# Planned attention, Fourier mixing and MLP on one core: the second batch's Y in other PSUM banks, fold scalings and some evacuations on ScalarE, tabled landing times for the loads

## The chip, the cores and the metric

The kernel runs on one core of a Trainium2 chip. The core has five engines with a queue each: TensorE (PE, matmuls, with its weight loads shown apart as PEld), VectorE (DVE), ScalarE (ACT), GpSimd (POOL) and SyncE (SP), which here only issues DMAs. An engine works through its queue in order; engines wait for each other through semaphores. TensorE writes to PSUM, which holds eight banks of 128 partitions x 512 fp32; DVE and ACT read the results out ("evacuate" them).

The metric is the device time in microseconds (us) of the whole kernel, the median over several runs. Seven runs of the kernel before gave 284.14 us as the median, from 281.46 to 285.59. One execution was profiled; it took 282.36 us, of which 280.6 us lie between its first and its last instruction (the span).

## The reference, cut to what matters

Four batches of 768 positions, 8 heads of 64. Attention keeps the first 8 keys and a band of 96; its output `x` is mixed by a two-dimensional Fourier transform of which only the real part is kept, normalised, and sent through a two-layer network:

```
scores = q @ k.T / 8 - slope[h] * dist        # kept: key < 8, or 0 <= i - j < 96
a      = softmax(scores)
x      = (a @ v), heads side by side            # 768 x 512 per batch
mixed  = real(fft(fft(x, axis=seq), axis=model))
u      = x + mixed
un     = (u - mean(u)) / sqrt(var(u) + 1e-6)
out    = u + relu(un @ w_ch1) @ w_ch2           # 512 -> 2048 -> 512
```

## The kernel before, in words

**Stages of a batch.** Eight heads are taken as four pairs `hp`; `n = 4*b + hp` counts pairs over all batches b = 0 to 3. For each pair q and k are loaded (`qs`), cast to fp16 (`qk`, line 398 on ACT, 402 on POOL), transposed on TensorE (`pt`, L487) and evacuated (`qkT`, L493, on DVE). Three score tiles follow (`sc_0` to `sc_2`, L529), each with an exponential on ACT (`er`, L552) and a product with the bias table on DVE (`ex`, L567). v is loaded by two DMAs a pair (`vs`, L360) and cast on POOL (L458). Six products with v (`pav`, L658) are normalised on DVE (L677 and L678) into `x`.

The Fourier transform over the sequence folds x first, on DVE: `f1` (L725, L726) forms sums and differences of the halves, `f2` (L731, L732) a second level, `f3` (L736 to L739) four of six results, the last two of them scalings by a constant, `f4` (L743, L744) the other two. `fold_d` folds over the model dimension: `g1` (L794 to L797) and `g2` (L811 to L822). The second batch's fold is cut into two halves of 256 columns, those of the third and fourth are whole (512). The folded tiles meet DFT matrices in `y_unit`: four groups of products (`py`, L855 to L862), each group in a PSUM tile of two banks, evacuated to `zy` (L875 on ACT, L877 on DVE). `mirror` makes reversed copies (`rev` on POOL, `ww` at L908 on ACT or L910 on POOL). `u_unit` makes three products (`pu`, L942) of pairs of row classes; DVE adds x (L963) and the row sums follow; `un` is the normalised row (L983 ACT, L985 DVE). `nt_unit` transposes it (`ptu`, L1014) and evacuates it (`unT`, L1024 ACT, L1026 DVE).

**The network.** Each batch gives three chunks `c` of 256 rows. A chunk has eight first products (`ph`, L1045, one bank each, evacuated with Relu into `hT` at L1051 on ACT or L1052 on DVE) and two second products (`pg`, L1068, four parts of four matmuls each), which end in `ob` (L1079, DVE) and a store (L1084, issued on ACT or SP).

**PSUM.** After the first batch's attention there are three rings: `xx` with two slots of two banks, for scores, transposes, pav, py, pu and ptu; `ph` with two single banks; `pg` with two single banks.

**What sets the order.** The program is written out by a planner (`Plan`) while it is built. It keeps a clock for each engine and a completion time for each token, in its own estimates (`act(n)`, `dve(n)`, `lat` for the landing of a load), and emits next what can start first, among `MIX`, `ATT`, `PH` and `PG` for TensorE and, for the other engines, among the operations that are ready. An operation with several "ways" goes to the engine that ends it earliest. The result is a fixed order on each queue. A wait that comes out longer on the chip than in the estimates holds everything behind it on that queue. An estimate that is changed moves instructions on all engines, though no operation is touched.

**Loads.** Loads of q and k rotate through three `qs` buffers, those of v through two. Until now a load's token was set to the planner's DMA clock plus a constant per batch: 4.5, 7.0 and 5.0 us for batches 1, 2 and 3.

Of the kernel before, what the change touches and what calls it, by code (L numbers as in the profile page):

```python
# [14 lines left out]
P = 128  # L15
# [160 lines left out]
def kernel(  # L176
# [48 lines left out]
    t0 = []  # L225
# [113 lines left out]
    qk16 = {}  # L339
    TT = {}  # L340

    def load(b, hp, which):
        n = HP * b + hp
        h0 = 2 * hp
        vtag, vi = ("u", hp) if b == 0 else ("vs", n - HP)
        stage[("vs", n)] = (vtag, vi)
        gate = [("hold", b)] if b == 2 else [("xri", 0)] if b == 1 else []
        if which == "v" and b == 0:
            def run():
                t = buf(vtag, vi, [P, 2 * NS, Dh], FP32, 1)  # L350
                stage[("v", n)] = t
                qk_dma(t.rearrange("p (j t) d -> p j (t d)", t=2), v, b, h0)
            pl.later([("SP", 0.45, run)], free(vtag, vi), 0.0, [("ld", "v", n)], dma=1.34)
        elif which == "v":
            def run():
                t = buf(vtag, vi, [P, 2 * NS, Dh], FP32, 1)
                stage[("v", n)] = t
                src = v[b, h0:h0 + 2].rearrange("h s d -> (h s) d").rearrange("(n m t) d -> t m n d", m=64, t=2)
                for t2 in range(2):
                    nc.sync.dma_start(t[64 * t2:64 * t2 + 64], src[t2])  # L360
            pl.later([("SP", 0.9, run)], free(vtag, vi) + gate, 0.0, [("ld", "v", n)], lat=(0.0, 4.5, 7.0, 5.0)[b], dma=2.45)
        elif b == 0 and hp < 3:
            cell = {}

            def run(cell=cell):
                cell[0] = buf("hT", hp, [P, 2, NS, 2 * Dh], FP32, 2)
                for w, src in enumerate((q, k)):
                    qk_dma(cell[0][:, w], src, b, h0)
            pl.later([("SP", 0.9, run)], free("hT", hp), 0.0, [("ld", "qk", n, w) for w in range(2)], dma=2.68,
                     then=lambda t: pl.tok.__setitem__(("ld", "qk", n, 0), t - 1.34))  # L370
            for w in range(2):
                cast_qk(b, hp, w, lambda w=w, cell=cell: cell[0][:, w], ("hT", hp))
        else:
            for w, src in enumerate((q, k)):
                cell = {}
                i = 2 * (n - 3) + w

                def run(cell=cell, src=src, i=i):
                    cell[0] = buf("qs", i, [P, NS, 2 * Dh], FP32, 1)
                    qk_dma(cell[0], src, b, h0)  # L380
                pl.later([("SP", 0.45, run)], free("qs", i) + gate, 0.0, [("ld", "qk", n, w)],
                         lat=(0.0, 4.5, 7.0, 5.0)[b], dma=1.34)
                cast_qk(b, hp, w, lambda cell=cell: cell[0], ("qs", i))

    def qk_dma(t, src, b, h0):
# [92 lines left out]
    def trans(b, hp):  # L478
        n = HP * b + hp

        def run(start, ring):
            pt = bank("xx", f"pt_{n}", FP16)
            src = qk16.pop(n)
            for w in range(2):
                for j in range(NS):
                    o = pt[:, w, (j // 2) * 256:(j // 2) * 256 + 256].rearrange("p (a t m) -> p t a m", a=2, t=2)
                    nc.tensor.transpose(o[:, j % 2], src[:, w, j].rearrange("p h d -> p (h d)"), idn)  # L487
            e = pl.pe(mm_us(P, 2 * NS), start)
            pl.used(("free", "qk", n), e)

            def evac():
                TT[n] = buf("qkT", n, [P, 2, S], FP16, 6)
                V.tensor_copy(TT[n], pt[:, :, 0:S])  # L493
            pl.later([("DVE", dve2(2 * S), evac)], free("qkT", n), e, [("qkT", n)], ring=ring, rank=RA(b))
            for s in range(2):
                def cp(s=s):
                    c0 = 16 * (hp % 2) + 8 * s
                    nc.gpsimd.tensor_copy(  # L498
                        kG[b % 2][64 * s:64 * s + 64, hp, c0:c0 + NG].rearrange("p (j m) -> p j m", j=2),
                        TT[n][64 * s:64 * s + 64, 1, 0:P].rearrange("p (j m) -> p j m", j=2)[:, :, 0:NG // 2])  # L500
                pl.later([("POOL", 0.2, cp)], [("qkT", n)] + ([("gldone", b - 2, hp // 2)] if b > 1 else []), 0.0,
                         [("kG", n, s)], [("free", "qkT", n)], rank=RA(b))
        ATT.append(([("qk", n, 0), ("qk", n, 1)], ("xx",), run))
# [205 lines left out]
    def fold_s(b):  # L709
# [5 lines left out]
        for n, (c0, cw) in enumerate(parts):  # L715
# [10 lines left out]
                VT(ab[:, 1], lo, hi, op=ALU.subtract)  # L726

            def f2(c0=c0, cw=cw, n=n, cell=cell):
                pm = cell["pm"] = buf("ww", IW(b, n), [P, 2, 2, cw], FP16, 1)
                ab = cell["ab"]  # L730
                VT(pm[:, 0], ab[:, :, 1], ab[:, :, 2], op=ALU.add)  # L731
                VT(pm[:, 1], ab[:, :, 1], ab[:, :, 2], op=ALU.subtract)  # L732

            def f3(c0=c0, cw=cw, cell=cell):
                ab, pm, zc = cell["ab"], cell["pm"], T[("z", b)][:, :, c0:c0 + cw]
                VT(zc[:, 0], ab[:, 0, 0], pm[:, 0, 0], op=ALU.add)  # L736
                VT(zc[:, 1], ab[:, 1, 0], pm[:, 1, 1], op=ALU.subtract)
                V.tensor_scalar_mul(zc[:, 4], pm[:, 1, 0], c)
                V.tensor_scalar_mul(zc[:, 5], pm[:, 0, 1], c)  # L739

            def f4(c0=c0, cw=cw, cell=cell):
                ab, pm, zc = cell["ab"], cell["pm"], T[("z", b)][:, :, c0:c0 + cw]
# [5 lines left out]
                     + (free("zy", 2 * b) if n == 0 else []), 0.0,  # L748
                     [("f1", b, n)], [("free", "x", b)] * (2 // len(parts)))
            pl.later([("DVE", 2 * dve2(2 * cw), f2)], [("f1", b, n)] + free("ww", IW(b, n)), 0.0, [("f2", b, n)])  # L750
            pl.later([("DVE", 4 * dve2(cw), f3)], [("f2", b, n)], 0.0, [("f3", b, n)])
            pl.later([("DVE", 2 * dve(cw), f4)], [("f3", b, n)], 0.0, [("z", b, n)],
                     [("free", "eA", IA(b, n)), ("free", "ww", IW(b, n))])
        return [("z", b, n) for n in range(len(parts))]

    def fold_s0():

# [85 lines left out]
    def y_unit(b, g, ts=None):  # L843
        def run(start, ring):
            py = bank(ring, f"py_{b}_{g}" + (f"_{ts[0]}" if ts else ""))
            cnt = 0
            ys = YG[g]
            for a, (rs, rd) in enumerate(ys):
                if ts and a // 2 not in ts:
                    continue  # L850
                o = py[:, a // 2, (a % 2) * 256:(a % 2) * 256 + 256]
                if b == 0:
                    ops = W[(0, rs, rd)]
                    for i, (l, r) in enumerate(ops):
                        nc.tensor.matmul(o, l, r, start=(i == 0), stop=(i == len(ops) - 1))  # L855
                    cnt += len(ops)
                    continue
                wr, wi = W[(b, rs, rd)]
                nc.tensor.matmul(o, wr, t1_sb[:, rs, 128:384], start=True, stop=(wi is None))  # L859
                cnt += 1  # L860
                if wi is not None:
                    nc.tensor.matmul(o, wi, t1_sb[:, rs, 0:256], start=False, stop=True)  # L862
                    cnt += 1
# [6 lines left out]
            def cp(on, lo, hi):  # L870
                if ("y", b) not in T:
                    T[("y", b)] = buf("zy", 2 * b + 1, [P, 8, 2, 2, P], FP16, 7)
                dst = T[("y", b)][:, 2 * g + lo:2 * g + hi].rearrange("p t a c m -> p t (a c m)")
                if on == "ACT":
                    A(dst, py[:, lo:hi, :], AF.Copy)  # L875
                else:
                    V.tensor_copy(dst, py[:, lo:hi, :])  # L877
                for t in range(lo, hi):
                    for a in range(2):
                        Y[(b,) + ys[2 * t + a]] = T[("y", b)][:, 2 * g + t, a]  # L880
            cuts = [(0, nb)] if ts is None else [(t, t + 1) for t in ts]
            for x, (lo, hi) in enumerate(cuts):
# [2 lines left out]
                          ("DVE", dve(w), lambda lo=lo, hi=hi: cp("DVE", lo, hi))],  # L885
                         free("zy", 2 * b + 1), e, [("y", b) + y for y in ys[2 * lo:2 * hi]],
                         CD(b) if x == len(cuts) - 1 else [], ring=ring if x == len(cuts) - 1 else None)
        MIX.append(([("w", b, 0 if g in (0, 3) else 1), ("c", "t1" if b else "t0")], BANKS(b), run))

    def mirror(b):  # L890

# [39 lines left out]
    def u_unit(b, pr):  # L931
# [4 lines left out]
        def run(start, ring):  # L936
# [29 lines left out]
                                           op0=ALU.mult, op1=ALU.add, accum_out=sm[:, a, 0:1])  # L966
                V.tensor_scalar_mul(sm[:, rows[0]:rows[-1] + 1, 1], sm[:, rows[0]:rows[-1] + 1, 0], -SC / Dm)

            cuts = [(0,), (1,)] if c == 0 else [(0, 1)]
            for rows in cuts:  # L970
                last = rows is cuts[-1]
                pl.later([("DVE", len(rows) * dve(512) + 0.15, lambda rows=rows: add(rows))],
# [4 lines left out]
            def un(on, a):  # L977

                if 0 not in cell:
                    cell[0] = T[("un", c)] = buf("un", 1 + c, [P, 2, Dm], FP16, 4 if c == 0 else 3)  # L980
                m = MV[c][:, a, 1:2]
                if on == "ACT":
                    A(cell[0][:, a], UT[c][:, a], AF.Identity, m, SC)  # L983
# [108 lines left out]
    with tc.manual_schedule():  # L1092
# [78 lines left out]
        for b in range(B):  # L1171
# [37 lines left out]
            bounce(b)  # L1209
            fold_d(b, fold_s(b))  # L1210
            for g in (0, 1, 2, 3):
                if b:
                    y_unit(b, g)
                    continue
                for t in range(len(YG[g]) // 2):
                    y_unit(b, g, [t])
                    if (g, t) == (2, 0):
                        u_unit(b, 0)
            mirror(b)
            if b:  # L1220
                u_unit(b, 0)
            u_unit(b, 1)
            for rows in ((0,), (1,)) if b == 0 else ((0, 1),):
                nt_unit(b, 0, rows)
            u_unit(b, 2)
            nt_unit(b, 1)
# [43 lines left out]
```

## Time and profile before

| what | value |
|---|---|
| median of 7 runs | 284.14 us (281.46 to 285.59) |
| profiled execution | 282.36 us, span 280.6 us |
| busy: PE, DVE, ACT, POOL | 265.1, 180.8, 145.7, 58.9 us |
| of it `ph` and `pg` matmuls | 95.1 and 90.7 us |
| chain that ended last | PE 78% of the span |
| granted TensorE clock | mean 0.991; 0.5 from 111.8 to 115.2 us |
| last matmul ends, span ends | 276.5 us, 280.6 us |

Busy PE is not PE at its peak: the ends of matmuls are modelled and overlap. What tells more is the time from one group of matmuls to the next. Undisturbed, eight `ph` matmuls take 0.87 us, four `pg` 0.86, sixteen `pu` 0.89, eight `ptu` 0.45, twelve `pt` 0.67 and four `sc` about 0.42. Where a group takes longer, or the next starts late, TensorE has lost time.

### The profile page before, as it was taken

How to read it: one execution, taken by the hardware profiler on the slowest of the kernel's cores; microseconds unless marked ns; L12 is line 12 of the kernel's file. 1: busy time of each engine (PE TensorE's matmuls, PEld its weight loads, DVE VectorE, ACT ScalarE, POOL GpSimd, SP SyncE). 2: the span in 40 equal slices, each digit the busy share in tenths (PEclk: the TensorE clock that was granted, in tenths of full speed). 3: DMA queues.
4: the chain of work that ended last, by engine and by line, in shares of the span. 5: the costliest groups of instructions: out<-in, count | busy, mean ns of one | idle time of the engine just before them, and what ended most of it. 6: DMA issues, size and time to landing. Idle time of an engine off the chain costs nothing.

```text
span 280.6 us, 6105 instructions
## 1 busy us (share of the span) xinstructions
PE 265.1 (94%) x2505; PEld 179.0 (64%) x2505; DVE 180.8 (64%) x363; ACT 145.7 (52%) x236; POOL 58.9 (21%) x115
## 2 busy tenths in 40 slices
PE   7788899899999996999999999999999899999994
PEld 3445587688675454776795576775866677767441
DVE  4675938677599978777899687575995672111121
ACT  2877347886741258668534267686142556434000
POOL 1572625154023323340111011111000120100000
PEclk9999999999999999799999999999999999999998
DMA  7999789999999999634047102000352010000111
GB/s 219 292 278 288 176 254 200 217 232 206 248 195 278 295 269 229 135 106 114 1 103 219 72 2 78 0 2 2 98 158 83 2 71 8 37 37 20 58 75 75
DMA packets 63101, 38.10 MB, mean 136 GB/s; under 512 B 20450, under 2 KB 58594, under 8 KB 62946
## 3 DMA queue, kind: packets, MB, share of 16 engines
q1 hardware_dynamic: 51458, 25.66, 38.4%
q10 hardware_dynamic: 7392, 7.87, 9.1%
q0 software_dynamic: 4224, 4.19, 9.1%
q8 instruction: 19, 0.31, 0.5%
q14 instruction: 8, 0.07, 0.1%
HBM read 32.47 MB, written 9.44 MB: 149 GB/s over the span
## 4 chain that ended last, share of the span: by engine, by line
PE 78%; SPq 7%; DMA 7%; DVE 4%; ACT 1%; issue 1%; ACTq 0%
PE ph L1045 31%; PE pg L1068 29%; SPq L387 5%; PE sc L529 4%; DMA qs<-in_q_dram 3%; PE pav L658 3%; PE pt L487 3%; DMA gb<-gbm 2%; PE pu L942 2%; PE ptu L1014 2%; DVE x L678 2%; PE py L859 2%; DVE u L963 1%; SPq L360 1%; PE py L862 1%; DMA xd<-x 1%
## 5 line engine op out<-in xcount | busy, mean ns | idle before, releaser
L1045 PE MATMUL ph<-unT,w 128*128 128x256 f16 x768 | 95.1, 274 | 1.1 <-ACT hT L1051 1.1
L1068 PE MATMUL pg<-w,hT 128*128 128x512 f16 x384 | 90.7, 379 | 0.0
L1045 PEld LDWEIGHTS <-w 128*128 128x128 f16 x768 | 71.9, 98 | 18.0 <-issue 6.9
L1068 PEld LDWEIGHTS <-hT 128*128 128x128 f16 x384 | 36.5, 98 | 35.7 <-issue 1.0
L1051 ACT ACTIVATE hT<-ph 128x512 f16<-128x512 f32 x60 | 35.7, 596 | 44.6 <-PE ph L1045 40.2
L552 ACT ACTIVATE er<-sc 128x992 f16<-128x992 f32 (+2 forms) x42 | 38.1, 924 | 14.2 <-PE sc L529 12.4
L1079 DVE SCALAR_TENSOR_TENSOR ob<-pg,sm,u 128x512 f32<-128x512 f32 x24 | 18.0, 750 | 37.7 <-PE pg L1068 34.5
L1052 DVE TENSOR_SCALAR hT<-ph 128x512 f16<-128x512 f32 x36 | 24.7, 689 | 19.4 <-PE ph L1045 19.4
L567 DVE TENSOR_TENSOR ex<-er,mk 128x992 f16<-128x992 f16 (+2 forms) x42 | 26.7, 652 | 2.3 <-ACT er L552 2.3
L398 ACT ACTIVATE qk<-qs 128x768 f16<-128x768 f32 x20 | 16.6, 838 | 17.7 <-DVE ob L1079 5.6
L963 DVE SCALAR_TENSOR_TENSOR u<-pu,xr 128x512 f32<-128x512 f32 x24 | 15.7, 687 | 8.7 <-PE pu L942 8.6
L493 DVE COPY qkT<-pt 128x1536 f16<-128x1536 f16 x16 | 15.3, 954 | 3.9 <-PE pt L487 3.7
L875 ACT ACTIVATE zy<-py 128x1024 f16<-128x1024 f32 (+1 forms) x11 | 9.1, 826 | 16.6 <-DVE eA L811 5.2
L678 DVE TENSOR_TENSOR x<-pav,rc 128x512 f16<-128x512 f32 (+1 forms) x27 | 17.1, 632 | 0.9
L529 PE MATMUL sc<-qkT 64*128 64x256 f16 (+1 forms) x192 | 16.8, 263 | 0.5 <-ACT v L449 0.4
L498 POOL COPY kG<-qkT 64x8 f16<-64x8 f16 x32 | 10.1, 316 | 33.1 <-DVE qkT L493 28.3
L658 PEld LDWEIGHTS <-ex 128*128 128x128 f16 x352 | 15.1, 97 | 2.2 <-DVE rc L677 0.4
L658 PE MATMUL pav<-v,ex 128*128 128x65 f16 x352 | 16.3, 193 | 0.0
L992 ACT ACTIVATE un<-un 128x512 f16<-128x512 f16 x24 | 14.9, 623 | 2.4 <-PE ptu L1014 2.4
L458 POOL CAST v<-vs 128x768 f16<-128x768 f32 x12 | 10.9, 908 | 16.7 <-DMA vs<-in_v_dram 16.4
L330 PE MATMUL fill<-eg 128*128 128x512 f16 x45 | 12.8, 435 | 1.4 <-DVE eg L1106 1.2
L487 PE MATMUL pt<-ident,qk 128*128 128x128 f16 x192 | 13.5, 219 | 0.6 <-POOL qk L402 0.4
(103 smaller groups left out, 283.0 us busy)
## 6 DMA issues: line engine op xcount, KB each, us to landing
qs<-in_q_dram SPq DMA_DIRECT2D x13, 384.0 KB, 6.4
qs<-in_k_dram SPq DMA_DIRECT2D x13, 384.0 KB, 6.7
vs<-in_v_dram SPq DMA_DIRECT2D x24, 192.0 KB, 6.9
w<-in_moe_w_ch_dram POOLq DMA_DIRECT2D x8, 512.0 KB, 9.5
out_dram<-ob ACTq DMA_DIRECT2D x12, 256.0 KB, 2.8
out_dram<-ob SPq DMA_DIRECT2D x12, 256.0 KB, 2.0
xd<-x ACTq DMA_DIRECT2D x12, 192.0 KB, 3.9
xr<-xd ACTq DMA_DIRECT2D x6, 384.0 KB, 3.9
```

Source lines behind the costliest of these rows:

```text
L487: nc.tensor.transpose(o[:, j % 2], src[:, w, j].rearrange("p h d -> p (h d)"), idn)
L529: nc.tensor.matmul(pa[:, s, c0:c0 + cw], TT[n][lo:lo + 64, 1, i * P:(i + 1) * P], TT[n][lo:lo + 64, 0, i * P:i * P + cw], start=(not inps) ...
L552: A(mine(), cut(pa), AF.Exp, 0.0, 0.125)
L567: VT(o, mine(), m, op=ALU.mult)
L658: nc.tensor.matmul(po[:, jj, hh * 65:(hh + 1) * 65], lhsT, v16[b % 2][:, i, h, 0:65], start=(jp == 0 and a == 0), stop=(a == len(ops) - 1) ...
L678: VT(X[b][:, 2 * jp:2 * jp + 2, first * Dh:(first + nh) * Dh].rearrange("p j (h d) -> p j h d", d=Dh), pv[:, :, :, 0:Dh], rc.to_broadcast( ...
L963: V.scalar_tensor_tensor(u[:, a].rearrange("p (n r) -> p n r", r=4), pu[:, a].rearrange("p (r n) -> p n r", r=4), 1.0, XR[b][:, (r0, r1)[a ...
L1045: nc.tensor.matmul(ph[:, a * CH:(a + 1) * CH], w1[:, d, jb * P:(jb + 1) * P], UNT[c][:, d, :], start=(d == 0), stop=(d == ND - 1))
L1051: pl.later([("ACT", act(512), lambda: A(dst, ph, AF.Relu)), ("DVE", dve(512), lambda: V.tensor_scalar_max(dst, ph, 0.0))], [], e, [("h", c ...
L1052: ("DVE", dve(512), lambda: V.tensor_scalar_max(dst, ph, 0.0))],
L1068: nc.tensor.matmul(pg, HT[c][:, jb, t * P:(t + 1) * P], w2[:, jb, :], start=(jb == 0), stop=(jb == NJ - 1))
L1079: V.scalar_tensor_tensor(cell[0], pg, MV[c][:, t, 3:4], UT[c][:, t, :], op0=ALU.mult, op1=ALU.add)
```

## The change

Four edits, and what follows from them in the planned order:

1. `y_unit` of batch 1 takes banks of the ring `ph` in place of `xx`. Each of its seven tiles is then a single bank with its own evacuation of 512 columns (before: three groups of 1024 columns and one of 512).
2. The two scalings of `f3` leave DVE and become two ACT operations (`f5`, token `z5`) for batches 1 to 3.
3. `trans` of batches 2 and 3 may evacuate `qkT` on ACT as well.
4. `LAND` gives the planner a completion time for every load of batches 1 and 2; `lat` changes for the rest.

Beside these, the first chunk's split into two rows of `u`, `un` and `ptu` is used for batch 1 too (before: batch 0 alone).

The counts of instructions that differ: DVE loses 8 scalings, 2 `qkT` copies and 3 `unT` copies of 1024 columns (it gains one of 512), its `zy` copies go from three of 1024 and five of 512 to one and eight, and it gains 4 `hT`. ACT gains the 8 scalings, 2 `qkT`, 2 `unT` of 1024 and one of 512, and loses 4 `hT` and 3 `ww` (to POOL); its `zy` copies go from six of 1024 and five of 512 to five and eight. TensorE has the same matmuls in another order.

```
@@ load
+    LAND = {4: (43.5, 43.3, 47.3), 5: (51.6, 55.5, 54.0), 6: (57.4, 60.9, 59.2), 7: (65.9, 67.0, 64.9),
+            8: (79.4, 81.6, 84.8), 9: (86.6, 91.0, 88.2), 10: (92.8, 96.3, 94.8), 11: (100.0, 102.5, 98.4)}
+    def landed(n, w):
+        def then(t):
+            if n in LAND:
+                key = ("ld", "v", n) if w == 2 else ("ld", "qk", n, w)
+                pl.tok[key] = max(pl.t["SP"] + 3.0, LAND[n][w])
+        return then
...
-            pl.later([("SP", 0.9, run)], ..., lat=(0.0, 4.5, 7.0, 5.0)[b], dma=2.45)
+            pl.later([("SP", 0.9, run)], ..., lat=(0.0, 4.0, 6.0, 5.0)[b], dma=2.45, then=landed(n, 2))
...
@@ trans
-            pl.later([("DVE", dve2(2 * S), evac)], ...)
+            pl.later([("DVE", dve2(2 * S), lambda: evac("DVE"))] + [("ACT", act(2 * S), lambda: evac("ACT"))] * (b > 1), ...)
...
@@ fold_s
-                V.tensor_scalar_mul(zc[:, 4], pm[:, 1, 0], c)
-                V.tensor_scalar_mul(zc[:, 5], pm[:, 0, 1], c)
+            def f5(c0=c0, cw=cw, cell=cell):
+                pm, zc = cell["pm"], T[("z", b)][:, :, c0:c0 + cw]
+                A(zc[:, 4], pm[:, 1, 0], AF.Copy, 0.0, c)
+                A(zc[:, 5], pm[:, 0, 1], AF.Copy, 0.0, c)
...
-            pl.later([("DVE", 4 * dve2(cw), f3)], [("f2", b, n)], 0.0, [("f3", b, n)])
+            pl.later([("ACT", 2 * act(cw), f5)], [("f2", b, n)], 0.0, [("z5", b, n)], [("free", "ww", IW(b, n))])
+            pl.later([("DVE", 2 * dve2(cw), f3)], [("f2", b, n)], 0.0, [("f3", b, n)])
...
@@ y_unit
-        MIX.append((..., BANKS(b), run))
+        MIX.append((..., ("ph",) if b == 1 else BANKS(b), run))
...
@@ order of the units of a batch
-                if b:
+                if b > 1:
                     y_unit(b, g)
                     continue
                 for t in range(len(YG[g]) // 2):
                     y_unit(b, g, [t])
...
-            for rows in ((0,), (1,)) if b == 0 else ((0, 1),):
+            for rows in ((0,), (1,)) if b < 2 else ((0, 1),):
                 nt_unit(b, 0, rows)
```

## The prediction

> **What bounds the kernel now.** First the busy time of the engines in stretches of 10 us (microseconds and number of instructions of PE, PEld, DVE, ACT, POOL, then granted clock, DMA share, GB/s):
>
> ```profile
> 40.00:50.00 10.00, 9.11 (x112) 7.26 (x110) 8.41 (x24) 6.75 (x13) 5.58 (x12) 1.00 1.20 216
> 80.00:90.00 10.00, 10.00 (x110) 6.04 (x107) 9.59 (x24) 1.69 (x2) 2.31 (x2) 1.00 1.20 252
> 90.00:100.00 10.00, 10.00 (x63) 5.12 (x62) 9.40 (x21) 3.46 (x4) 3.39 (x4) 1.00 1.04 292
> 100.00:110.00 10.00, 9.16 (x83) 5.96 (x82) 7.04 (x16) 6.61 (x11) 3.20 (x7) 1.00 1.09 235
> 110.00:120.00 10.00, 8.50 (x86) 6.46 (x83) 7.99 (x17) 6.52 (x11) 4.05 (x7) 0.83 0.76 169
> 210.00:220.00 10.00, 8.93 (x65) 5.60 (x64) 5.16 (x10) 4.23 (x6) 0.86 (x3) 1.00 0.19 76
> ```
>
> From 51 us to the last matmul at 276.5 TensorE is full, but for 104 to 120 and 210 to 220. Before 80 to 100, where the second batch folds, DVE is full and ACT mostly free. After 50 us the time is TensorE's work plus its holes, so I asked next what its matmuls waited for between 40 and 230 us (total, times, longest):
>
> ```profile
> PE ptu L1014 <- DVE u L963: 1.5, 1, 1.5
> PE ph L1045 <- ACT hT L1051: 1.1, 1, 1.1
> PE pu L942 <- ACT un L983: 0.8, 1, 0.8
> PE ptu L1014 <- ACT un L983: 0.6, 1, 0.6
> PE pu L942 <- ACT zy L875: 0.6, 1, 0.6
> PE pu L942 <- DVE zy L877: 0.5, 1, 0.5
> ```
>
> These are all the holes there are. The chain of work shows where they come from, at 50 us and at 110 us (start, duration, what):
>
> ```profile
> 40.85 8.64 DMA qs<-in_q_dram
> 50.27 0.59 ACT hT L1051
> 50.90 1.03 PE ph L1045 x8
> ...
> 108.20 1.22 DVE u L963 x4
> 109.54 0.75 DVE ob L1079
> 110.29 0.39 DVE un L985
> 110.68 1.29 DVE u L963 x4
> 112.11 1.86 PE ptu L1014 x16
> 114.41 1.40 PE ph L1045 x8
> ```
>
> At 50 us a load of q that landed at 49.5 holds ACT's queue with `hT` behind it. At 110 us TensorE has used up the first batch's ph and pg and waits for DVE to free one of the two `xx` slots. Then sixteen `ptu` take 1.86 us for 0.89 and eight `ph` 1.40 for 0.87: the clock is at 0.5 from 111.8 to 115.2.
>
> **Base of the sum.** The profiled execution took 282.36 us, 1.78 under the median of 284.14. Savings are taken from 282.36; the 1.78 is added at the end. The changed order is known (positions of instructions, no times); I walked it with durations of this trace.
>
> **Hole 1, 50 us: 1.1 us.** Up to 45.5 us the order of TensorE is unchanged. Then `ph_0` moves ahead of `pu`; both orders reach the end of `ptu` at 48.40, so `ph_1` fills 48.40 to 49.27 and `ph_2` wants the bank of `ph_0`. ACT before it: two `un` to 43.2, a cast 0.83, `ww` 0.54, `unT` of 512 (new on ACT, 0.6), square 0.8, `ww`, square: 47.3, then `hT` of `ph_0` to 47.9. In time by 1.3. The cast of the next q (landing 49.5) now stands behind `hT` of `ph_0`, a `unT` of 1024 (1.02) and `hT` of `ph_1`, so the 1.1 us go. What is new: SP issues q of pair 6 ahead of k of pair 5; these change places, so k lands near 55.6 instead of 53.3. ACT reaches its cast at 55.2 and has a `unT` of 1.02 behind it: done at 57.5, when the `pt` that needs both stands at 57.9. Cover 0.4 us; if it is gone the loss is the lateness, 0 to 1 us. I take 0.
>
> **Hole 2, 104 to 120 us: 4.0 us.** From `pg` at 107.38 to `pt` at 115.64 are 8.26 us for 0.86 pg + 0.41 sc + 0.89 pu + 0.89 ptu + 0.33 sc + 0.87 ph = 4.25. What the change leaves of it:
>
> *The fold on DVE.* The third product with v is normalised to 82.05 in both. First half: f1 1.0, `ob` 0.66, f2 0.8, f3 without its scalings 0.41, f4 0.75, then two norms of 0.85 and `ob`: norms end at 88.2 and the last one at 89.05 (before 89.41). Second half: f1 1.0, f2 0.8 to 1.3 (one of its two took 0.93 beside a POOL copy, against 0.43), `ob` and f3 to 92.55, f4 to 93.3. Before there followed a `qkT` copy of 0.87; that one is on ACT now. So g1 starts at 93.3 to 93.8 against 94.86, its Y can be multiplied from 95.3 to 95.8 and stands at 96.6 in TensorE's order; g2 is done near 98.7 (before 99.6) and stands at 100.6. Both have over 0.8 us of cover.
>
> *ACT's share.* Two scalings per half: on DVE the pair took 0.27 (start to start 0.13 and 0.14 of rows of 0.22). ACT has no such row; its nearest, copies of 512 columns SBUF to SBUF, take 0.618 (0.52 start to start). The Trainium skill, "ScalarE: Activation LUTs", section "Rules for kernel authors", speaks against this edit: multiplications belong on VectorE, up to three times faster per element. By the same page (186 ns plus 0.833 ns per element) a scaling of 256 costs about 0.40 us as an estimate, 0.8 for two against 0.27: by the rule alone the edit loses 0.5 us per half. The rows decide, because DVE is 96% and 94% busy here and ACT 17% and 35%: on the path it saves 0.27 per half. It costs nothing while `z5` is done before g1. In ACT's queue the second pair stands behind two `xd` issues (to 90.35) and the new `qkT` of 1536 columns, which I put at 1.43 (rows: 512 in 0.597, 1024 in 1.016): 91.8, scalings to 92.5. Cover 0.8.
>
> *What queues on ACT.* Behind them: a cast, a store's issue, then the `xr` issue, which waits for `xd` (written 5 us earlier: 95.0), two `er`, a cast of k, a store that waits for `ob`: the first two Y copies end at 99.65 and 100.25. The `ph` banks they free are wanted at 100.6 and 101.1. Without that cover TensorE stops one for one.
>
> *Slots.* Y no longer passes through `xx`, so `pu` goes at 104.5 instead of 105.6, and row-wise `u` lets `un` start at 106.75 instead of 108.24. By DVE's order (four Y copies to 105.35, `ex`, `u` with sums to 107.45, `u` to 108.85, half a `unT`, `ob` 110.1, `un` 110.5, `unT` 110.95) the last `ptu` gets its slot at 110.95 and would have gone at 110.3; some 0.15 is lost at `pu`. New loss 0.8 us, bounds 0.3 and 3.1.
>
> *Clock.* The skill, "TensorE: Matmul & The Clock Gate", section "HAM oscillation — how this bites in real kernels", warns of idle gaps over about 3.4 us. Here gaps of 0.84 and 1.50 us, 2.3 us of the 3.4 before 111.8, were enough: the measurement decides. By the rule hole 2 would be only 2.3 us of idling; by the rows 1.6 of its 4.0 are half clock and go too, if the gaps go. With gaps of 0.8 I expect full clock. Saved: 4.0 − 0.8 = 3.2.
>
> **Third batch, 130 to 165 us: 0.** No hole before; TensorE reaches it 4 to 5 us earlier. `pav` ends near 136.2, norms 137.5, f1 1.9 to 2.5, f2 1.2, `hT`, f3, f4, `qkT`: 144.5, g1 to 146.5 for Y at 149.7; g2 149.0 for 150.6; on ACT the second `qkT` ends 145.9, for a score at 146.7. Covers of 0.8 or more; where they fail the gain is given back.
>
> **Hole 3, 216 us: 1.4 us.** `pu` waited 0.6 for a Y copy on DVE and 0.8 for one on ACT: the last Y groups stood right in front of it. Now two `ph` stand between the first and the other Y, and `pu` follows another `pg`: `py_1` ends 206.4 on the moved clock, its DVE copy (1.23) 207.7, `pu` stands at 207.9. `py_2` is copied on ACT to 207.9 and mirrored to 208.9, wanted at 209.6. Fold of that batch: g1 done 201, wanted 202.7. Saved 1.4.
>
> **The rest: 0.** All stages from 228 us on and the 4.1 us after the last matmul are the same. The other `hT`, `ww` and `vG` that change engine lie beside TensorE's work.
>
> Sum: 282.36 − 1.1 − 3.2 − 1.4 = 276.66; plus 1.78: **278.4 us**, 2.0% below the median.
>
> **Rivals.**
> *A, as worked out: 278.4* (277.2 to 279.4), chance 0.55.
> *B, the hole moves but stays:* the second batch ends late by slot and ACT order, 0.8 plus a gap as large plus the half clock (1.6): 3.1 lost instead of 0.8. For it: covers of 0.4 at ACT's copies and the tie of slots at 109 to 111. Against: all its parts are earlier than before. 280.7, chance 0.2.
> *C, more than A:* without gaps no execution drops its clock, and the spread of 4.1 us between runs narrows to its lower end: 276.4, chance 0.08. The profile of one run can't show it.
> *D, many small waits* at covers of 0.4 (57, 100, 109, 137, 153 us), each 0.5 to 1, together 4: 282.4, chance 0.1.
> *E, slower:* the table of landings is wrong. A cast of pair 11 stands in ACT's queue in front of the Y copies at 100 us; tabled 102.5 for its k, which landed at 103.3 before; the planner's clock runs some 2 us ahead (pair 5's q: tabled 51.6, landed 49.5). Casts now free the `qs` buffers earlier, which speaks against it. Landing at 102 costs 0.5. Every us after that is a us of TensorE, with 1.6 for each drop of the clock. From a landing near 107 the gain is gone; at 110 with one more drop: 288, chance 0.07.
>
> One per cent, 2.8 us, is about what a measurement of this kernel can tell from no change. A, C and three quarters of B lie below 281.3: faster 0.78; D and the rest of B 0.15; slower 0.07. The range leaves out E, the low end of C and the upper part of D: 275.8 to 282.0.
>
> **What would show it.** Waits of PE between 40 and 230 us: no `ph <- hT` of 1.1, `ptu` and `pu` waits together about 1 instead of 4; granted clock 1.00 in every stretch from 50 to 270; first `ph` of the second batch near 111.4 instead of 114.3; last matmul near 270.8. Wrong if ACT is found waiting on a `qs` landing or on `xd` with `zy` behind it, if a clock row below 1 remains, or if the hole of the second batch comes back at 150 to 165.

## The result, and the profile after

The changed kernel takes 280.3 us (median of 12 runs, 278.82 to 283.94), the kernel before beside it 283.84 us (median of 31 runs). The ratio is 0.9885 with a 95% interval from 0.9852 to 0.9918: 1.1% faster, where 2.0% were forecast. Here and below the ratios leave out executions more than 1.5% above the fastest of the same kernel, so they are not quite the quotients of the medians. A second comparison with other runs gave 281.6 us and 0.9932 (0.9896 to 0.9968). By the one the gain is 3.3 us, by the other 1.9, of a forecast of 5.7.

The profiled execution took 278.82 us (span 277.0), 3.5 less than that of before; it is the fastest of the 12. Busy time in stretches of 10 us, columns as before:

```profile
40.00:50.00 10.00, 7.98 (x97) 6.54 (x94) 7.18 (x20) 6.79 (x13) 5.54 (x11) 1.00 1.13 205
70.00:80.00 10.00, 8.55 (x90) 5.48 (x90) 6.35 (x11) 8.33 (x13) 0.73 (x2) 1.00 1.10 208
100.00:110.00 10.00, 10.00 (x96) 6.59 (x96) 9.70 (x19) 8.11 (x13) 4.79 (x9) 1.00 1.16 270
110.00:120.00 10.00, 9.62 (x103) 7.47 (x102) 9.29 (x24) 9.20 (x16) 3.76 (x5) 1.00 1.14 237
210.00:220.00 10.00, 10.00 (x90) 6.25 (x88) 5.98 (x15) 4.79 (x9) 1.47 (x4) 1.00 0.07 28
```

The rows that were forecast to fill are full, or nearly so: 100 to 120 us and 210 to 220, with the clock at 1.00. Two others are not: 40 to 50 lost more than before (7.98 against 9.11), and 70 to 80, full before, has a hole. What TensorE waited for between 40 and 230 us, all that the profile lists:

```profile
PE pt L498 <- ACT er L566: 1.8, 1, 1.8
PE pt L498 <- ACT unT L1045: 1.4, 1, 1.4
PE ptu L1035 <- ACT un L1004: 0.6, 1, 0.6
PE ptu L1035 <- DVE unT L1047: 0.3, 1, 0.3
```

Gone are the waits for `hT`, `u` and the Y copies. New are two of `pt` for ScalarE. The chain of work from 40 to 75 us says what ScalarE waited for (start, duration, what):

```profile
35.78 8.44 DMA qs<-in_k_dram
...
45.60 0.49 ACT unT L1045
46.09 0.04 issue
46.14 0.83 PE pt L498 x12
...
58.69 10.96 DMA qs<-in_k_dram
...
70.42 0.99 ACT er L566
71.41 0.04 issue
71.45 0.83 PE pt L498 x12
```

In both places a load of k lands late, its cast stands in ScalarE's queue, and behind the cast stand operations whose data had long been there: at 46 us the `unT` that frees an `xx` slot, at 71 us two `er` that free another. From group to group TensorE lost 1.5 us at 46 and 1.9 us at 71.

So the 3.5 us are made of: 1.1 at 50 us, 3.3 at 104 to 120, 1.4 at 216, and 0.8 by which everything before 42 us ran earlier in this execution with the order unchanged there (the `ptu` at 42.7 us in the trace of before comes at 41.8 to 43.0 in the 14 traces of this study, so this part is chance); less 1.5 and 1.9. That is 3.2; the rest are smaller differences.

### The profile page after: what moved, and what is told of

Read it like the earlier page. It is cut to its first block, busy times and chain, and to the rows that moved or that the text cites. A ratio compares the mean times of both kernels' runs of the same rounds, so it can differ in the third digit from the quotient of the medians.

```text
span 277.0 us, 6109 instructions
## 1 busy us (share of the span) xinstructions
PE 263.1 (95%) x2505; PEld 177.9 (64%) x2505; DVE 177.5 (64%) x356; ACT 151.1 (55%) x245; POOL 61.1 (22%) x118
## 4 chain that ended last, share of the span: by engine, by line
PE 75%; DMA 11%; DVE 5%; SPq 3%; issue 2%; POOL 1%; ACT 1%; ACTq 0%; POOLq 0%
PE pg L1089 29%; PE ph L1066 28%; DMA qs<-in_k_dram 7%; PE sc L543 4%; PE pav L672 3%; PE pt L498 3%; DMA qs<-in_q_dram 2%; PE pu L963 2%; SPq L398 2%; DVE x L692 2%; PE ptu L1035 2%; PE py L879 2%; PE py L882 1%; DMA xd<-x 1%; PE pav L661 1%
## 5 line engine op out<-in xcount | busy, mean ns | idle before, releaser
L1066 PE MATMUL ph<-unT,w 128*128 128x256 f16 x768 | 93.9, 273 | 0.0
L1089 PEld LDWEIGHTS <-hT 128*128 128x128 f16 x384 | 35.9, 98 | 35.7 <-issue 1.5
L1072 ACT ACTIVATE hT<-ph 128x512 f16<-128x512 f32 x56 | 33.4, 597 | 46.4 <-PE ph L1066 46.2
L1073 DVE TENSOR_SCALAR hT<-ph 128x512 f16<-128x512 f32 x40 | 27.6, 690 | 17.3 <-PE ph L1066 17.0
L896 ACT ACTIVATE zy<-py 128x512 f16<-128x512 f32 (+1 forms) x13 | 9.7, 760 | 11.4 <-DVE eA L829 5.2
L498 PEld LDWEIGHTS <-qk 128*128 128x128 f16 x192 | 11.6, 98 | 6.1 <-issue 3.6
L507 DVE COPY qkT<-pt 128x1536 f16<-128x1536 f16 x14 | 13.4, 954 | 2.6 <-PE pt L498 2.4
```

What stands on the lines that cost most here:

```text
L1066: nc.tensor.matmul(ph[:, a * CH:(a + 1) * CH], w1[:, d, jb * P:(jb + 1) * P], UNT[c][:, d, :], start=(d == 0), stop=(d == ND - 1))
L1072: pl.later([("ACT", act(512), lambda: A(dst, ph, AF.Relu)), ("DVE", dve(512), lambda: V.tensor_scalar_max(dst, ph, 0.0))], [], e, [("h", c ...
L1073: ("DVE", dve(512), lambda: V.tensor_scalar_max(dst, ph, 0.0))],
L1089: nc.tensor.matmul(pg, HT[c][:, jb, t * P:(t + 1) * P], w2[:, jb, :], start=(jb == 0), stop=(jb == NJ - 1))
```

## The experiments

My theory after the traces: the Y banks, the fold and the order around them removed the waits they were expected to remove, and the fourth edit, the table of landings, brought the two new ones. The rival: the table carries the gain.

### The two new waits, one at a time, with the order kept

Pair 4's casts change engines; the weight load of the second layer, first quarter, is issued with the second quarter:

```diff
 def cast(on):                   # cut
+    if n == 4:
+        on = "POOL" if w else "ACT"
```

```diff
 def wload(i):                   # cut
+    if i == 4:
+        return
+    if i == 5:
+        wdma(4)
+    wdma(i)
```

The weight load was a suspect because of GpSimd's timeline (start, duration, what). Before:

```profile
60.78 1.57 POOL L1159 DMA_DIRECT2D w<-in_moe_w_ch_dram  x2
```

and after, where the cast of v of pair 6 comes earlier, and the first weight load right behind it:

```profile
57.17 0.83 POOL L469 CAST v<-vs 128x768 f16<-128x768 f32 x1 [0.62 <-DMA vs<-in_v_dram]
57.93 0.82 POOL L1180 DMA_DIRECT2D w<-in_moe_w_ch_dram  x1
```

The load of k of pair 7, on SP, is issued at 58.08 us before, and after at

```profile
58.69 1.04 SPq L398 DMA_DIRECT2D qs<-in_k_dram  x1
```

so the weight load has passed it.

> The changed kernel with one exchange and every queue's order kept: the casts of q and k of pair 4 change engines (q on ScalarE, k on GpSimd, each in the other's place). q landed at 41.81 us and k at 44.22, so ScalarE has nothing to wait for at 42.5 and GpSimd takes the wait. Theory (the late k held ScalarE's queue, and with it the unT that frees the slot for pt): pt of pair 4 starts near 45.1 us in place of 46.14, its wait falls from 1.4 us to about 0.4, and the median goes from 280.3 to about 279.3 (ratio to the kernel before 0.985). Rival (the data are late, whoever casts them, and something else stands behind): the wait stays at 1.0 to 1.5 us or comes back as a wait for the second ww on GpSimd, now 2.3 us later; 280.3 or more.

Measured: 281.72 us, ratio 0.9922 (0.9883 to 0.996). The waits of TensorE no longer have the one at 46 us, but the one at 71 us has grown:

```profile
PE pt L500 <- ACT er L568: 2.7, 1, 2.7
```

Counted from the first `ptu` (42.96 us here, 41.96 in the changed kernel's trace), k of pair 7 lands after 27.7 us in both. TensorE now comes to it 0.9 us earlier and waits 0.9 us longer; and after this longer wait the clock fell (0.83 in the row of 70 to 80). The mechanism at 46 us was as expected, the saving was not: it was given back 25 us later, and in this execution the clock took some 1.5 us more.

> The changed kernel with one DMA issued later and every other instruction in its place: the first quarter of the second layer's weights is issued with the second quarter (near 60.7 us) in place of 57.9, so that the load of k of pair 7 (issued at 58.7) goes ahead of it, as in the kernel before. Theory (this weight load, moved ahead of k by the landing table, made k land 11.0 us after its issue in place of 7.0, and ScalarE's cast of it held the two er behind it): k lands at 65 to 67 us in place of 69.65, the wait of pt for er near 71 us (1.8) is gone, and the median is about 278.4 (ratio 0.981). Rival (the same bytes are in flight in either order, or another queue holds k): k still lands after 69 us, the wait stays, 280.3.

Measured: 279.81 us, ratio 0.9891 (0.9839 to 0.9942). k landed at 64.65 us, 5.6 after its issue in place of 11.0. The wait at 71 us is gone, that at 46 is there as expected, and there is a new one; the two largest:

```profile
PE ptu L1035 <- ACT un L1004: 3.9, 2, 3.2
PE pt L498 <- ACT unT L1045: 1.3, 1, 1.3
```

So the weight load was the cause of the wait at 71 us. But the profiled execution (282.19 us) lost the time elsewhere; the chain of work near 111 us:

```profile
100.16 11.24 DMA qs<-in_q_dram
...
112.27 0.62 ACT un L1004
112.89 0.05 issue
112.93 0.40 PE ptu L1035 x4
```

The cast of q of pair 12 holds `un`, TensorE waits 3.2 us, and its clock is 0.83 in the row of 110 to 120. The median was forecast at 278.4.

> Both of the two edits before it. Theory: both new waits of TensorE are gone, savings add up: 1.0 + 1.9, about 277.4 us (ratio 0.977), and no granted clock below 1.00 from 50 us on. Rival (TensorE is early and runs into the next limit, the second batch's fold on VectorE at 95 to 110 us): the gain of one or of both is lost again by 115 us, seen as a larger wait of pu or ptu there; 279 to 280.

Measured: 279.17 us, 276.99 at the lowest, ratio 0.9856 (0.9787 to 0.9925). The profiled execution took 276.99: no wait above 0.6 us is left from 40 to 230 us, and the clock is 1.00 throughout.

```profile
PE ptu L1037 <- ACT un L1006: 0.6, 1, 0.6
PE ptu L1037 <- DVE unT L1049: 0.3, 1, 0.3
...
```

That is close to the prediction's sum for a profiled execution (276.66): with these two waits gone, the rest of the change does what was forecast. It is one execution, the fastest of six that reach up to 285.48, and the interval overlaps those of the changed kernel: what the two waits cost is shown by the traces, not by the medians.

### The table, taken out and put in alone

> The changed kernel without its fourth edit: no table of landings and the constants of the kernel before; the other three edits stay. Theory (Y in the ph banks, the row split and the fold on ScalarE removed the waits at 104 to 120 and 216 us; the table removed the wait at 50 us and made those at 46 and 71): the first product of the second batch starts as early against its predecessors as in the changed kernel, waits at 46 and 71 are gone (1.5 + 1.9), the one of hT near 50 us is back (1.1): about 278 us (ratio 0.980). Rival (the table carries the gain, since it alone moves the casts and the copies on ScalarE around the fold): ptu waits 1.5 us or more near 110 us again and the clock drops; 283 to 284 (ratio 1.00).

Measured: 280.03 us, ratio 0.9879 (0.9826 to 0.9932), the same as with the table.

```profile
PE ph L1056 <- ACT hT L1062: 2.3, 1, 2.3
PE py L869 <- DVE zy L888: 1.6, 1, 1.6
```

The waits at 46 and 71 us are gone, and two others are there: that for `hT` near 50 us is back, now 2.3 in place of 1.1, and `py` waits 1.6 at 108. I had expected 278: the 2 us are the larger `hT` wait, a drop of the clock behind it (0.5 from 52.9 to 56.3 us), and the wait at 108. Against the other three edits alone the table is worth nothing that can be measured: it trades two waits for two.

> The kernel before with the fourth edit alone (the table of landings and its constants). Theory (the table gives back what it takes): a wait for ScalarE's cast of a late k at 46 or at 71 us or at both in place of the hT wait at 50, the waits of ptu and pu at 104 to 120 us as before; 283 to 286 (ratio 0.997 to 1.007). Rival (the table carries the gain): 280 to 281 (ratio 0.987 to 0.990), with ptu and pu waits near 110 us at 1 us or less.

Measured: 287.29 us, ratio 1.0108 (1.0065 to 1.015). The waits show what the table brings by itself (two of `pt`, at 72.7 and 46.2 us); the waits of the kernel before near 110 and 220 us stay beside them (not shown):

```profile
PE pt L497 <- ACT er L562: 3.0, 1, 3.0
...
PE pt L497 <- ACT unT L1034: 1.1, 1, 1.1
```

The rival has fallen. The loss is larger than the 0.7% that I had allowed at most; the clock is at 0.5 twice in this trace, from 73.2 and from 114.2 us, for 3.4 us each.

### The other three edits, each taken back

> The changed kernel without its first edit: Y of the second batch in the xx slots again, in groups of two banks, and its first chunk not split by rows; table, ScalarE scalings and qkT on ScalarE stay. Theory (the xx slots that Y holds make the second batch's pu, ptu and unT late): ptu and pu together wait 2.5 us or more between 104 and 120 us, with a clock row below 1.00 there; about 283.5 (ratio 0.998). Rival (the fold's place on VectorE, not the slots, set that wait): waits there stay near 1 us; 280.3 (ratio 0.9885).

Measured: 283.43 us, ratio 0.9987 (0.9948 to 1.0026): the time is as expected, the trace only in part. From 110 to 120 us `ptu` waits 0.8 and a score 1.3, both for `u` on VectorE, and the clock stays at 1.00 there; the 71 us wait was 3.1 in this execution. Against the profiled execution of the changed kernel TensorE stands 1.7 us later by 75 us, from that wait and the drop of the clock behind it, and 3.3 later at the end. So by this trace about half of the difference comes from a load and 1.6 us arises later, where the edit is; that the median agrees with the expectation does not show its mechanism.

> The changed kernel with all qkT copies on VectorE. Theory (one copy of 0.87 us goes ahead of g1 in the second batch's fold, whose cover was put at 0.8): g1 0.9 us later, wait of TensorE 0 to 0.3; median within 0.7 us of 280.3 (ratio 0.987 to 0.991). Rival (this copy is what made the fold early enough): py waits about 1 us near 96 us and ptu or pu as much again near 110; 282 (ratio 0.994).

Measured: 282.44 us, ratio 0.9957 (0.9924 to 0.9991), nearer to the rival. g1 starts at 98.1 us, 2.3 later than in the changed kernel's trace. Some 1.6 of these come from the waits before it (the one at 71 us was 2.5 here and the clock fell behind it, worth some 1.6; the one at 46 was shorter), which leaves 0.7 for the copy. `py` waits for nothing, as expected; a `ptu` waits 1.3 at 114.8 for a `unT` on ScalarE, which was not. This edit's share can't be told from that of the clock by one trace.

> The changed kernel with the two scalings of each fold back on VectorE. Theory (0.27 us on VectorE per half or whole fold, beside a cover of 0.8 us): g1 and g2 of the second batch come 0.3 to 0.6 us later against TensorE, no wait of py for them; the median stays within 0.5 us of 280.3 (ratio 0.987 to 0.990). Rival (VectorE at 94 to 96% has no cover): the products wait for eA or ww of the fold, 1 us or more near 95 to 105 us; 281.5 or more (ratio 0.992).

Measured: 287.25 us, ratio 1.0122 (1.0073 to 1.0171), 7 us from what I expected and far beyond the rival.

```profile
PE pt L498 <- ACT er L566: 2.8, 1, 2.8
PE pu L959 <- DVE u L980: 1.6, 1, 1.6
...
PE pu L959 <- DVE zy L894: 0.9, 2, 0.5
```

The second half's `f1` starts at 95.44 us here and at 91.48 in the changed kernel: in the planned order its last norm comes at 93.3 (90.8), and a `qkT` copy and an `ob` stand between. g1 starts at 101.0 in place of 95.8, and by 113 TensorE has run out of other work. The two `pu` waits of 0.5 are at 165 and 219 us. Some of the delay comes on top of the order: two of the fold's operations took twice their time beside casts on GpSimd (last section), 1.2 us. To part the engine from the order, the scalings were executed on VectorE at the places that the planner had given them on ScalarE:

```diff
-    A(zc[:, 4], pm[:, 1, 0], AF.Copy, 0.0, c)
-    A(zc[:, 5], pm[:, 0, 1], AF.Copy, 0.0, c)
+    V.tensor_scalar_mul(zc[:, 4], pm[:, 1, 0], c)
+    V.tensor_scalar_mul(zc[:, 5], pm[:, 0, 1], c)
```

> The changed kernel with the eight scalings executed on VectorE, each at the place in the order that the planner gave it for ScalarE; every other instruction keeps its engine and its place. Theory (the 7 us of the run with the scalings replanned onto VectorE came from the order that followed, its second half-fold began at 95.4 us in place of 91.5): VectorE pays 0.27 us per half, g1 of the second batch starts at about 96.0 in place of 95.8, no wait of pu at 165 or 219 us; 280.3 to 281 (ratio 0.9885 to 0.991). Rival (VectorE's time itself is what matters): pu waits again near 110 and 219 us, 284 or more (ratio 1.00 or above).

Measured: 282.14 us, ratio 0.9943 (0.9902 to 0.9983), against 281.6 and 0.9932 for the changed kernel in the same comparison. The waits of TensorE, all of them:

```profile
PE pt L498 <- ACT er L566: 2.8, 1, 2.8
PE pt L498 <- ACT unT L1045: 1.3, 1, 1.3
PE ptu L1035 <- ACT un L1004: 0.6, 1, 0.6
PE ptu L1035 <- DVE unT L1047: 0.3, 1, 0.3
```

None is at 165 or 219 us (the 0.6 is at 42), and near 110 there is only the one of 0.3. g1 was expected at 96.0 and starts at 99.8: of the 4.0 us to the changed kernel's 95.8, 3.0 stand before the fold begins (87.5 in place of 84.5: a later start, the longer wait at 71 us and the clock behind it), 1.0 arises in it. Even so no wait follows from it. The engine makes half a us by the medians, less than the intervals can tell; the 5 us between the two kernels are the order, with what runs beside what in it.

> The changed kernel once more, beside the two others, for a second profile of it and for the comparison. Theory: the waits of pt at 46 us (1.0 to 1.6) and at 71 us (1.5 to 3) are there again; median 280.3 within 1 (ratio 0.985 to 0.992). Rival (they were an accident of one execution): one or both are below 0.5.

Measured: 281.6 us, ratio 0.9932 (0.9896 to 0.9968). Both waits of `pt` are there again, 1.1 and 1.8; they belong to the order, not to one execution. A score waits 0.8 at 101 us for ScalarE's `er`, which it did not in the first profile.

### What lies behind: the loads

The third edit on top of the first two defers one cast:

```diff
 def cast(on):                   # cut; the load of k of pair 13 moves too
+    if (n, w) == (12, 0):
+        held.append(lambda: put(on))
+        return
+    if (n, w) == (12, 1):
+        while held:
+            held.pop(0)()
+    put(on)
```

> The changed kernel with the exchange of pair 4's casts, the later weight load, and a third edit that keeps the order else: the cast of q of pair 12 goes in ScalarE's queue behind the three un and one ww that it stood in front of, right ahead of the cast of k of the same pair (the load of k of pair 13, which takes over its buffer, is issued one place later on SP). Theory (a cast that waits for a load holds un in some executions, 1.3 to 4.5 us near 109 us in the traces so far, and this makes most of the spread): no wait of ptu for ScalarE's un above 0.6 near 110 us; median about 277.5 (ratio 0.977), highest below 280. Rival (the spread comes from elsewhere, or the buffer that is freed later makes the next loads late): 279 or more, or waits of pt for casts at 117 to 125 us.

Measured: 278.78 us, ratio 0.9812 (0.9751 to 0.9872), 276.17 at the lowest, the lowest median of this study: its interval lies below that of the changed kernel in the same comparison. It has six executions; over all of them the quotient of the medians is 0.984. The deferred cast did its part: in the profiled execution no `ptu` waits over 0.4 us near 110. But the executions reach from 276.17 to 284.24 us, so this cast does not make most of the spread, and there the rival was right. The profiled execution is a long one (282.71 us): `pt` waits 4.3 us near 71 again. There the weight load followed k by 1.41 us, where in the two kernels before it had been 2.0.

That distance, taken from every trace of this case (issue of the first weight load less issue of k of pair 7, and k's time from issue to landing), sorts the executions:

| kernel | distance, us | k's landing, us |
|---|---|---|
| before, no table | 2.70, 2.72 | 7.0, 4.3 |
| weight load later; both edits | 2.04, 2.03 | 5.6, 6.7 |
| three holds | 1.41 | 12.8 |
| Y in `xx`; `qkT` on VectorE; scalings there, replanned and in the old places | 0.17, -0.07, -0.25, -0.29 | 12.0, 11.7, 12.0, 12.0 |
| weights behind v of pair 7 (below) | 5.50 | 6.6 |
| casts exchanged, table alone, change twice | -0.01, -0.14, -0.76, -0.64 | 11.9, 12.2, 11.0, 11.0 |

With a lead of 2 us or more k landed in at most 7; with 1.4 or less it landed within 0.7 us of the second weight load. Between 1.4 and 2.0 us there is no trace, so a lead of 2.0, as the weight load's edit gives, may be near the edge. The last kernel moves both weight loads behind the cast of v of pair 7:

```diff
 def run():                      # cast_v, cut
     nc.gpsimd.tensor_copy(...)
+    if n == 7:
+        second.extend((4, 5))
+        while second:
+            wl[0](second.pop(0))
```

> The kernel with three holds removed, its weight loads moved once more: the first two quarters of the second layer's weights are issued behind GpSimd's cast of v of pair 7 (near 63.2 us) in place of 60.7, all else in its place. In the traces so far k of pair 7 landed 5.6 to 7.0 us after its issue where the first of these weight loads followed it by 2.0 us or more, and 11 to 12.8 us after it, together with the second weight load, where it followed by 1.4 us or less or went ahead. Theory (this distance decides): it is 4 us now; k lands before 67 us, pt waits less than 0.5 us near 71, no clock row below 1.00 near 72; median about 277.3 (ratio 0.977). Rival (k's landing varies by itself, or the weights now come too late for the loads behind them): a wait of 1.5 us or more at 71 us, or a new one where pair 8's q and k are cast (80 to 95 us); 279 or more.

Measured: 280.68 us, ratio 0.9889 (0.9826 to 0.9953). k lands at 64.35 us, both early waits are below 0.5, TensorE is over 3 us ahead of the changed kernel at 75 us, and then it runs into the loads of the third batch (chain of work; the second load is pair 11's q):

```profile
94.45 10.45 DMA qs<-in_q_dram
...
105.82 0.50 ACT zy L919
106.32 0.04 issue
106.36 0.37 PE py L902
```

`py` waits 2.8 us, and the clock falls.

This is rival E's place in the prediction, a cast of pair 11 in front of the Y copies. What was won by 75 us was lost by 110. Whether those loads were late because the weights went later was not tried. The trace shows one link: SP issues the loads of the third batch behind a small DMA (`hold`) that waits for the second of these weight loads, so they begin at 72.92 us here and at 69.92 in the changed kernel. Why q of pair 11 then took 10.45 us from issue to landing (4.1 to 7.4 in the other traces that show it) stays open.

## Why the prediction was right or wrong

**The number.** The median, 280.3 us, is 1.9 above the forecast of 278.4 and inside its range. That is in part luck: the two new waits, 3.4 us, stood in no step of the sum, and the range was wide for other reasons. B's 280.7 is nearer, but what B described, a hole that stays at 110 us, did not come.

**Hole 1, 50 us: the wait went, the time did not.** The failing step is "Up to 45.5 us the order of TensorE is unchanged" with "two `un` to 43.2, a cast 0.83": it took for granted that k of pair 4 was there at 43.2. It landed at 44.22. It was as late before: no view of that trace gives its landing, but the last signal of its 16 DMA engines comes at 44.14, and ScalarE reached its cast only at 44.44, behind that of q and a `ww`, so nobody waited for it. The table has k at 43.3, ahead of q at 43.5, though q is issued first and landed 2.4 us ahead of k; I did not question that. Saved 1.1, paid 1.5.

**The swap of q of pair 6 and k of pair 5: right.** k landed at 54.95 (put at 55.6), and TensorE lost nothing at 57.

**What was missing: GpSimd's queue.** I followed the loads that change places on SP, not the weight load on GpSimd that passes k of pair 7. No step of the sum has it; it put nothing for 71 us, and 1.9 were lost there. With the first miss that makes 3.4 us; less the 0.8 that came from the start and some 0.4 of small differences it is the 2.2 between the forecast 276.66 and the profiled 278.82.

**Hole 2: right.** 0.8 us forecast, 0.7 found (0.2 at `pu`, 0.5 at `ptu`, on VectorE's `unT`), and the clock at 1.00. The new `qkT` on ScalarE took 1.45 us (estimate 1.43). A scaling of 256 took 0.41 there (0.40 as an estimate by the price in the Trainium skill, "ScalarE: Activation LUTs", "What ACT_TABLE_LOAD costs") against 0.22 on VectorE: the page's price holds. The advice of its "Rules for kernel authors", multiplications on VectorE, does not decide here, since with the order kept the engine hardly matters. g1 came at 95.8 us, not at 93.3 to 93.8, late by the two new waits; the cover of Y over it, 0.8, was as forecast. What I had wrong is the edit's worth: 0.27 us per half was my whole account of it, and replanned without it the kernel loses 7.

**Clock.** In the prediction's 2.3 us of the 3.4 before 111.8, the second gap is counted whole; it ends at 112.11, so 2.0 us lie in them. The conclusion, full clock with gaps of 0.8, held.

**Third batch 0 and hole 3, 1.4: right.** No wait is listed from 120 to 230 us. Waits near 219 us came back in two kernels with another order, the table alone and the scalings replanned.

**The marks.** First `ph` of the second batch at 113.87 (forecast 111.4), last matmul at 273.0 (270.8). Both are late by the two new waits less the early start. Of the signs of being wrong one came, in another place: ScalarE stood idle 1.7 us up to 44.2 and 2.6 up to 69.7 for a landing of `qs`, with `unT` and `er` behind it, not `zy`.

**Rivals.** C said that without gaps no execution drops its clock and the spread narrows. The gaps only moved, and the spread did not narrow: 278.82 to 283.94 us. Of the 12 runs six have a mean clock of 0.997 or more, with spans of 277.0 to 277.9; the six at 0.985 to 0.994 have 279.1 to 282.1. With both waits removed the executions still reach from 276.99 to 285.48. D and E were under-weighted: their mechanism, a cast that waits for a load with TensorE's next release behind it, sits at 46, 71, 106 or 111 us in one trace or another. E's 1.6 us for a drop of the clock was about right: it cost 1.4 to 1.6 behind the waits at 71 us, by how much later TensorE stood after it.

## What to carry to other kernels

When an edit moves an order, list every DMA issue that it moves on every queue, and put no cast that waits for a load in front of an operation that frees something for the engine that bounds. An edit's own price and the price of the order that a planner makes of it are two numbers: here half a us and five. And a saved wait is kept only if the next load is early enough: with the DMA share at 1.0 or above in nearly every row from 40 to 120 us, that was to be seen before.

## What the runs showed that was not expected

A load of 384 KB issued 1.4 us or less ahead of two weight loads of 512 KB from another queue, or just behind the first, landed together with the second of them, 11 to 13 us after its issue, and in 4 to 7 us with a lead of 2.0 us or more (14 traces).

The clock fell to 0.5 behind single waits of TensorE of 2.3 us (at 50), 2.5 to 3.1 (at 71, five traces), 2.8 (at 106) and 3.2 (at 111), each time for 3.4 us, and for 6.8 behind the one of 4.3 (at 71). It did not fall behind waits of 1.8, and in one trace (scalings replanned) not behind one of 2.8. Where a wait lies in time explains that one. From the first rise of the clock, 4.0 to 7.2 us after the start, up to its drop after the last matmul, every stretch at one clock in the 14 traces lasts a whole multiple of 3.413 us; in the kernel before they are 105.8, 3.4 and 163.8, which is 31, 1 and 48 times that. Cut a trace into these steps, and each fall from full clock follows a step in which TensorE was idle for 2.0 to 3.1 us, once for 1.7; after every other step, with 1.75 us of idling at most, the clock stayed. The wait of 2.8 us that cost nothing lay across the border of two steps, with 1.3 us in the one and 1.5 in the other; of the two gaps in the kernel before, 2.0 us lay in one. As the steps begin elsewhere in each execution, the same wait can cost 1.5 us in one and nothing in the next. The 3.4 us of the Trainium skill ("TensorE: Matmul & The Clock Gate", "HAM oscillation — how this bites in real kernels") are not a bound for a gap to rely on here.

Some of VectorE's sums and differences took about twice their time beside GpSimd's casts: in the kernel with the scalings replanned onto VectorE, the second operation of `f1` and that of `f2` in the second half took 1.18 and 1.04 us in place of 0.55 and 0.42, next to casts of v that ran from 95.4 and 97.1 us. The first operation of each, which also ran beside the cast, took its usual time.
